# Scatters tied to evictions, a PSUM copy moved to ScalarE and output adds moved later, in a convolution and expert kernel

## The chip, the cores and the metric

The kernel runs on one core of one Trainium2 chip. The metric is the device time of one execution in microseconds. A comparison runs the kernel and the kernel before in turn on the same chip. What differed is the chip, or something that goes with a call on it, and this turned out to matter more than the change: the same kernel before takes about 1382 us in some calls and 1474 to 1501 us in others. On chip 13 it took about 1477 us in both calls; no other chip is known to have been used twice, so chip and call are not fully told apart, and "chip" below stands for either. Absolute times are therefore compared only inside one batch of runs, and ratios only between chips of the same kind.

## The reference

Tokens are 8 sequences of 3584, 192 channels wide. First comes a causal convolution of seven taps with softmax weights, one set for each of eight heads. Then every token goes to one of eight experts: the arg max of its logits, or the expert of the token before if a local gate is 0.5 or more. Output and arithmetic are float32.

```python
h = np.maximum(x[b, s] @ w1[e], 0.0)      # 192 -> 1024
out[b, s] = p[e] * (h @ w2[e])            # 1024 -> 192, times the softmax share
```

## The kernel before

The tokens are cut into 16 groups of 14 x 128. For each group VectorE does the convolution, a *gate round* on TensorE finds the logits, VectorE works out a slot for each token, and 14 *scatters* (indirect DMAs issued by GpSimd) put the rows into a buffer in DRAM, sorted by expert. TensorE works through *blocks* of that buffer: one unit (128 tokens) for the first 35 blocks, then two units, then one unit again. A block is: hidden matmuls, relu, transposes of the next block's tokens, output matmuls into two PSUM tiles, their sum times the gate, and one indirect DMA to the output for each unit.

The parts that the change touches:

```python
def put():                       # one scatter
    ...
    ins = nc.gpsimd.indirect_dma_start(out=slots[:, :], in_=rows, ...)

def turn(n, xg):                 # transposes on TensorE into xps, then
    nc.vector.tensor_copy(to..., at...)        # xT <- xps, on VectorE
    return xT

def output(n, wb, xg, hT):
    ...                          # matmuls into yps[0], yps[1]
    for k in range(n):
        nc.scalar.activation(o_sb[:, k, :], y[0], Act.Copy, scale=gate)
        nc.vector.scalar_tensor_tensor(o_sb[:, k, :], y[1], gate, o_sb[:, k, :],
                                       Alu.mult, Alu.add)
        ...                      # indirect DMA to out

def step(time, scatters):        # a share of the next groups' convolution or routing,
    ...                          # put into the engines' queues here
    for _ in range(scatters):
        put()

for i, (_, n, _, _) in enumerate(blocks):
    ...
    hT = hidden(n, wbs[i], xT)
    if i + 1 < len(blocks):
        xT = turn(blocks[i + 1][1], xgs[i + 1])
    step(2.5 if n == 1 else 4.2, 1)
    output(n, wbs.pop(i), xgs.pop(i), hT)
    step(2.5 if n == 1 else 4.2, n)
```

`step` hands out routing work up to a "hop", where an answer of another engine is needed. The rest of that step is convolution, and the next step goes on after the hop.

## Time and profile before

| | kernel before |
|---|---|
| time, 3 runs without a profile | 1381.68 us (1381.24 to 1384.63) |
| span of the profiled execution | 1474.5 us |
| busy: TensorE, weight loads | 94%, 89% |
| busy: VectorE, ScalarE, GpSimd | 61%, 29%, 33% |

Shares of the span do not say what is worth changing here; the kernel has four stretches with different limits, and the prediction below reads them one by one. The first oddity is the table itself: the profiled execution is 93 us longer than the timed ones.

### The profile page before, as it was taken

To read this page: it belongs to the slowest core of one execution; us is meant where nothing else is said; L and a number is where in the kernel's file an instruction comes from. 1 tells how busy PE (TensorE), PEld (TensorE's weight loads), DVE (VectorE), ACT (ScalarE), POOL (GpSimd) and SP (SyncE) were. 2 spreads that over 40 slices of the span, in tenths; PEclk is the share of its full clock that TensorE was granted. 3 is DMA by queue.
4 is the path that set the end of the run, shared out by engine and by line. 5 is a ranking of instruction groups with operands and counts; after the bars stand their busy time and mean duration, and the time that the engine had idled before them with its cause. 6 is when DMAs were issued, how large, how long until landed. Compare 5 with 4: busy or idle time off the path is not lost.

```text
span 1474.5 us, 41949 instructions
## 1 busy us (share of the span) xinstructions
PE 1393.4 (94%) x17314; PEld 1315.6 (89%) x17314; DVE 896.7 (61%) x2605; ACT 434.6 (29%) x1014; POOL 479.3 (33%) x515
## 2 busy tenths in 40 slices
PE   6689999999999999999999999999999999999998
PEld 4379888889898999898989999899989999999998
DVE  7579888887777878777777777777531111111111
ACT  3223323323233323232332323232222222222332
POOL 1332434333334333333434343434334212111111
PEclk9789999999999999999999999999999999999999
DMA  4397988885656565656565656555556655546894
GB/s 168 137 345 309 349 335 322 318 319 211 246 199 243 208 247 209 240 203 243 202 246 194 250 192 246 199 185 199 186 199 207 216 180 190 199 166 242 315 325 145
DMA packets 66480, 344.13 MB, mean 233 GB/s; under 512 B 12528, under 2 KB 23655, under 8 KB 45810
## 3 DMA queue, kind: packets, MB, share of 16 engines
q1 hardware_dynamic: 44064, 288.76, 55.0%
q0 software_dynamic: 22224, 52.70, 9.4%
q8 instruction: 136, 2.23, 0.6%
q14 instruction: 54, 0.44, 0.1%
q10 hardware_dynamic: 2, 0.00, 0.0%
HBM read 288.61 MB, written 53.49 MB: 232 GB/s over the span
## 4 chain that ended last, share of the span: by engine, by line
PE 58%; issue 23%; DVE 8%; POOL 5%; DMA 2%; another core or an unknown queue 2%; ACT 1%; POOLq 0%; DVEq 0%; SPq 0%; ACTq 0%
PE yps L756 26%; PE hps L741 24%; POOL out_dram L770 4%; DVE y_sb L206 3%; PE hps L350 3%; PE xps L278 2%; POOL slots L566 1%; PE yps L189 1%; PE hps L189 1%; DMA wb<-in_w_dram 1%; DVE xT L727 1%; DVE o_sb L766 1%; DMA out_dram<-o_sb,xg 1%; DMA x_sb<-in_x_dram 0%
## 5 line engine op out<-in xcount | busy, mean ns | idle before, releaser
L756 PE MATMUL yps<-wb,hT 64*128 64x192 f32 x7392 | 672.4, 327 | 23.2 <-issue 19.1
L756 PEld LDWEIGHTS yps<-wb,hT 64*128 64x128 f32 x7392 | 615.3, 188 | 48.4 <-issue 42.7
L741 PE MATMUL hps<-xT,wb 64*128 64x256 f32 (+1 forms) x6912 | 643.0, 337 | 7.8 <-DVE xT L727 5.0
L741 PEld LDWEIGHTS hps<-xT,wb 64*128 64x128 f32 x6912 | 608.6, 188 | 21.8 <-DVE xT L727 9.5
L770 POOL DMA_INDIRECT out_dram<-o_sb,xg x231 | 234.9, 1017 | 854.6 <-DVE o_sb L766 782.8
L206 DVE SCALAR_TENSOR_TENSOR y_sb<-x_sb,c,y_sb 128x336 f32<-128x336 f32 x720 | 402.9, 568 | 20.3 <-ACT y_sb L181 2.5
L746 ACT ACTIVATE hT<-hps 128x512 f32<-128x512 f32 (+1 forms) x576 | 264.9, 510 | 432.6 <-PE hps L741 317.4
L566 POOL DMA_INDIRECT slots<-y_sb,posi x224 | 217.4, 971 | 112.7 <-issue 108.4
L765 ACT ACTIVATE o_sb<-yps,xg 128x192 f32<-128x192 f32 x231 | 87.6, 418 | 503.0 <-PE yps L756 492.4
L766 DVE SCALAR_TENSOR_TENSOR o_sb<-yps,xg,o_sb 128x192 f32<-128x192 f32 x231 | 87.9, 412 | 240.8 <-ACT o_sb L765 233.5
L724 DVE COPY xT<-xps 128x768 f32<-128x768 f32 x87 | 82.8, 952 | 193.4 <-remote 107.6
L278 PEld LDWEIGHTS xps<-ident,xg 64*128 64x128 f32 x1386 | 78.0, 140 | 3.4 <-PE hps L741 0.3
L278 PE MATMUL xps<-ident,xg 64*128 64x64 f32 x1386 | 77.0, 223 | 0.1
L727 DVE COPY xT<-xps 128x384 f32<-128x384 f32 x57 | 31.6, 554 | 64.8 <-PE xps L278 47.3
L181 ACT ACTIVATE y_sb<-x_sb,c 128x336 f32<-128x336 f32 x116 | 64.7, 575 | 0.0
L350 PE MATMUL hps<-z,wg 64*32 64x128 f32 x1344 | 44.7, 286 | 16.0 <-issue 15.7
L350 PEld LDWEIGHTS hps<-z,wg 64*32 64x32 f32 x1344 | 25.5, 110 | 32.0 <-issue 31.1
L366 DVE COPY lt<-lq 32x36 f32<-32x36 f32 x224 | 44.6, 199 | 3.3
L340 DVE STREAM_TRANSPOSE z<-y_sb 128x768 f32<-128x768 f32 (+1 forms) x56 | 44.1, 844 | 0.0
L189 PE MATMUL hps<-x_sb,wb 128*128 128x336 f32 x56 | 17.8, 482 | 3.5 <-DMA x_sb<-in_x_dram 3.5
L189 PEld LDWEIGHTS hps<-x_sb,wb 128*128 128x128 f32 x56 | 11.5, 207 | 9.4 <-issue 4.8
L355 ACT COPY ls<-hps 128x128 f32<-128x128 f32 x28 | 6.1, 269 | 46.7 <-PE hps L350 46.7
(166 smaller groups left out, 367.3 us busy)
## 6 DMA issues: line engine op xcount, KB each, us to landing
wb<-in_w_dram SPq DMA_DIRECT2D x144, 1536.0 KB
x_sb<-in_x_dram SPq DMA_DIRECT2D x16, 1920.0 KB
xg<-slots SPq DMA_DIRECT2D x87, 258.0 KB
xg<-slots SPq DMA_DIRECT2D x57, 129.0 KB
out_dram<-o_sb,xg POOLq DMA_INDIRECT x231
slots<-y_sb,posi POOLq DMA_INDIRECT x224
wg<-in_wgl_dram SPq DMA_DIRECT2D x1, 144.0 KB
slots<-pad SPq DMA_DIRECT2D x1, 129.0 KB
```

Source lines behind the costliest of these rows:

```text
L181: nc.scalar.activation(cols(h), chans(h, 0), Act.Copy, scale=c[:, h, 0:1])
L206: nc.vector.scalar_tensor_tensor(cols(h), chans(h, k), c[:, h, k:k + 1], cols(h), Alu.mult, Alu.add)
L278: nc.tensor.transpose(to, src[rows], identity=ident[rows, rows])
L350: nc.tensor.matmul(lps[half][Q * j:Q * j + Q, :], lhsT=wgq[rows, b, :], rhs=z[rows, begin[j]:begin[j] + TQ, b * Q:(b + 1) * Q], start=(b = ...
L566: ins = nc.gpsimd.indirect_dma_start(out=slots[:, :], in_=rows, in_offset=None, out_offset=bass.IndirectOffsetOnAxis(ap=to, axis=0)).ins
L724: nc.vector.tensor_copy(to.rearrange("p h d k s -> p h (d k) s"), at.rearrange("p h d k s -> p h (d k) s"))
L741: nc.tensor.matmul(hps[half][:, j, w], lhsT=wb[rows, f0:f0 + P], rhs=xT[rows, d, w], start=(d == 0 and j == 0), stop=(d == KD - 1), skip_g ...
L746: nc.scalar.activation(hT[:, m:m + 2, w], hps[half][:, :, w], Act.Relu)
L756: nc.tensor.matmul(yps[half][:, k * D:(k + 1) * D], lhsT=hT[rows, m, k * P:(k + 1) * P], rhs=wb[rows, WA + m * D:WA + (m + 1) * D], start= ...
L765: nc.scalar.activation(o_sb[:, k, :], y[0], Act.Copy, scale=gate)
L766: nc.vector.scalar_tensor_tensor(o_sb[:, k, :], y[1], gate, o_sb[:, k, :], Alu.mult, Alu.add)
L770: sent = nc.gpsimd.indirect_dma_start(out=out, in_=o_sb[:, k, :], in_offset=None, out_offset=bass.IndirectOffsetOnAxis(ap=xg.bitcast(I32)[ ...
```

## The change

Its intent is to keep GpSimd from issuing many scatters in a row, to take the copy off VectorE, and to let VectorE do convolution work while ScalarE evicts the first half of the output. Cut to its core:

```diff
-    def put():
+    def put(behind=None):
...
+        if behind is not None:
+            tc.add_manual_dep(ins, behind.ins.name, SYNC, reason="scatters apart")
...
-            nc.vector.tensor_copy(...)
+        copied = nc.scalar.copy(to, at)
+        return xT, copied
...   # hidden(), after each of the two pairs of relus
+            put(relu)
...   # output()
         for k in range(n):
-            nc.scalar.activation(o_sb[:, k, :], y[0], Act.Copy, scale=gate)
-            nc.vector.scalar_tensor_tensor(o_sb[:, k, :], y[1], gate, o_sb[:, k, :],
+            nc.scalar.activation(o_sb[:, k, :], y[k][0], Act.Copy, scale=xg[:, k, 0:1])
+        step(1.2)
+        for k in range(n):
+            nc.vector.scalar_tensor_tensor(o_sb[:, k, :], y[k][1], ...)
...   # main loop
-            xT = turn(blocks[i + 1][1], xgs[i + 1])
-        step(2.5 if n == 1 else 4.2, 1)
+            xT, copied = turn(blocks[i + 1][1], xgs[i + 1])
+            if len(to_put) > NT // 2 and n == KT:
+                put(copied)
+        step(2.5 if n == 1 else 4.2)
         output(n, wbs.pop(i), xgs.pop(i), hT)
-        step(2.5 if n == 1 else 4.2, n)
+        step(1.3 if n == 1 else 3.0)
```

More of the change, by code (lines that the diff above doesn't have):

```diff
@@ L723, in turn @@
         if n == KT:
-            nc.vector.tensor_copy(to.rearrange("p h d k s -> p h (d k) s"),
-                                  at.rearrange("p h d k s -> p h (d k) s"))
-        else:
-            nc.vector.tensor_copy(to[:, :, :, 0, :], at[:, :, :, 0, :])
-        return xT
+            to, at = [a.rearrange("p h d k s -> p h (d k) s") for a in (to, at)]
+        else:
+            to, at = [a[:, :, :, 0, :] for a in (to, at)]
+        copied = nc.scalar.copy(to, at)
+        return xT, copied
     def hidden(n, wb, xT):
@@ L745, in hidden @@
                 m = half * 4 + two * 2
-                nc.scalar.activation(hT[:, m:m + 2, w], hps[half][:, :, w], Act.Relu)
+                relu = nc.scalar.activation(hT[:, m:m + 2, w], hps[half][:, :, w], Act.Relu)
+            put(relu)
         return hT
@@ L761, in output @@
         o_sb = op.tile([P, KT, D], F32, name="o_sb")
+        y = [[yps[half][:, k * D:(k + 1) * D] for half in range(2)] for k in range(n)]
         for k in range(n):
-            gate = xg[:, k, 0:1]
-            y = [yps[half][:, k * D:(k + 1) * D] for half in range(2)]
-            nc.scalar.activation(o_sb[:, k, :], y[0], Act.Copy, scale=gate)
-            nc.vector.scalar_tensor_tensor(o_sb[:, k, :], y[1], gate, o_sb[:, k, :],
+            nc.scalar.activation(o_sb[:, k, :], y[k][0], Act.Copy, scale=xg[:, k, 0:1])
+        step(1.2)
+        for k in range(n):
+            nc.vector.scalar_tensor_tensor(o_sb[:, k, :], y[k][1], xg[:, k, 0:1], o_sb[:, k, :],
                                            Alu.mult, Alu.add)
@@ L809, in route_op, with step @@
         return c
-    def step(time, scatters):
+    def step(time):
         start_route()
@@ L830, in step @@
                 time -= c
-        for _ in range(scatters):
-            put()
     start_conv(ON_PE)
@@ L870, in ensure @@
                     return
-                step(4.2, 1)
+                step(4.2)
+                put()
             xgs[j] = load_rows(j)
@@ L885 @@
     weights(AHEAD - 1)
-    xT = turn(blocks[0][1], xgs[0])
+    xT, _ = turn(blocks[0][1], xgs[0])
     for i, (_, n, _, _) in enumerate(blocks):
```

## The prediction

> **What bounds the kernel now.** I read the page first, then a table of stretches, then timelines of single blocks. The page's span is 1474.5 us, but the runs without a profile take 1381.68 us: the profiled execution is 93 us longer. Which of its stalls belong to the kernel and which to being profiled is therefore the main question.
>
> The stretches, cut where the blocks change (one unit per block from 80.7 us on, two units with scatters from 321.1, two units without from 1152.2, one unit again from 1346.6). Columns after the stretch: length, busy time (and count) of TensorE matmuls, weight loads, VectorE, ScalarE, GpSimd, then granted clock, DMA share, GB/s.
>
> ```profile
> 80.70:321.10 240.40, 224.91 (x3400) 209.57 (x3402) 202.97 (x584) 78.93 (x220) 92.08 (x93) 0.97 0.89 331
> 321.10:1152.20 831.10, 801.08 (x9520) 758.94 (x9518) 591.44 (x1764) 242.72 (x521) 307.92 (x309) 1.00 0.61 216
> 1152.20:1346.60 194.40, 194.40 (x2231) 193.89 (x2229) 30.20 (x54) 52.25 (x108) 36.00 (x37) 1.00 0.54 188
> 1346.60:1474.50 127.90, 121.57 (x1889) 120.97 (x1885) 21.65 (x45) 38.94 (x112) 23.33 (x24) 0.99 0.75 268
> ```
>
> In the third stretch TensorE has no gap. A block of two units there, from the TensorE timeline:
>
> ```profile
> 1206.26 5.39 PE L741 MATMUL hps<-xT,wb 64*128 64x256 f32 x48
> 1211.44 0.58 PE L278 MATMUL xps<-ident,xg 64*128 64x64 f32 x12
> 1211.81 5.47 PE L756 MATMUL yps<-wb,hT 64*128 64x192 f32 x64
> 1217.07 3.23 PE L741 MATMUL hps<-xT,wb 64*128 64x256 f32 x28
> ```
>
> From start to start it takes 1217.07 - 1206.26 = 10.81 us; the same reading for one unit (1413.23 to 1418.74) gives 5.51 us. These are the floors. The second stretch has 69 two-unit blocks, x 10.81 = 746 us, and ten rounds of gate matmuls (960 of them, 30.7 us busy). The remainder, about 54 us, is stalls. They look like this (a block where VectorE has no other work at all, so that only scatters can matter):
>
> ```profile
> 1095.07 0.98 POOL L770 DMA_INDIRECT out_dram<-o_sb,xg  x1 [5.71 <-DVE o_sb L766]
> 1096.35 0.98 POOL L770 DMA_INDIRECT out_dram<-o_sb,xg  x1 [0.30 <-issue]
> 1097.64 0.97 POOL L566 DMA_INDIRECT slots<-y_sb,posi  x1 [0.30 <-issue]
> ...
> 1098.91 0.96 POOL L566 DMA_INDIRECT slots<-y_sb,posi  x1 [0.30 <-issue]
> ...
> 1100.17 0.96 POOL L566 DMA_INDIRECT slots<-y_sb,posi  x1 [0.30 <-issue]
> 1102.11 3.25 PEld L756 LDWEIGHTS yps<-wb,hT 64*128 64x128 f32 x40 [0.82 <-issue]
> 1102.12 3.53 PE L756 MATMUL yps<-wb,hT 64*128 64x192 f32 x40 [0.39 <-issue]
> 1102.19 0.96 DVE L724 COPY xT<-xps 128x768 f32<-128x768 f32 x1 [7.07 <-remote]
> ```
>
> Five indirect DMAs in a row, then TensorE's weight loads miss 0.82 us and the copy of the transposed tokens, whose transposes ended near 1099.6, starts at 1102.19. That block takes 11.7 us. Blocks with two output DMAs and no scatter keep 10.81. This is what the diff aims at.
>
> But do the runs without a profile have those stalls? Add the floors: 80.7 us of start + the second stretch at its floor, 746 + 10 x 2.5 = 771 us + the last two stretches, 194.4 + 127.9 = 322.3 us. That is 1174 us and leaves 1381.7 - 1174 = 208 us for the first stretch, which needs at least 35 x 5.51 = 193 us of blocks and about 4 x 2.5 = 10 us of gate matmuls, 203 us. The runs without a profile thus have room for next to none of the 54 us; even if the start is 10 us shorter there, only some 15 us are free. I read most of the stalls as brought by the profile.
>
> The first stretch is different: there VectorE is busy 203 of 240 us, and a block is its work. Its timeline over one block:
>
> ```profile
> 95.62 2.85 DVE L206 SCALAR_TENSOR_TENSOR y_sb<-x_sb,c,y_sb 128x336 f32<-128x336 f32 x5
> 95.76 2.95 PE L741 MATMUL hps<-xT,wb 64*128 64x128 f32 x48
> ...
> 98.39 0.41 DVE L766 SCALAR_TENSOR_TENSOR o_sb<-yps,xg,o_sb 128x192 f32<-128x192 f32 x1
> ...
> 98.72 2.85 DVE L206 SCALAR_TENSOR_TENSOR y_sb<-x_sb,c,y_sb 128x336 f32<-128x336 f32 x5
> ...
> 101.49 0.55 DVE L727 COPY xT<-xps 128x384 f32<-128x384 f32 x1
> ...
> 102.09 2.95 PE L741 MATMUL hps<-xT,wb 64*128 64x128 f32 x48 [0.37 <-issue]
> ```
>
> TensorE starts the next block at 102.09, just when the copy ends at 102.04. The period, 6.33 us, is VectorE's queue: 2.85 + 0.41 + 2.85 + 0.55 less overlaps. The copy stands last in it.
>
> **The Trainium skill.** "Perfetto Trace Analysis", section "Identifying the Most-Contended Engine", says matmul busy share overstates TensorE and weight-load share is fairer: here 759 of 831 us in the second stretch against 193.9 of 194.4 in the third, so the scattered stretch does have gaps in the profile. "ScalarE: Activation LUTs", section "What ACT_TABLE_LOAD costs", gives 186 ns + 0.833 ns per element for an ACTIVATE with immediates: 826 ns for 768 elements and 506 for 384. The trace has 595 ns for 512 and 381 for 256 (the relus), a few per cent less than the formula's 612 and 399, so I take 810 and 490 ns. "DMA: Bandwidth & Descriptors", section "Specifications", puts the HBM limit per core near 358 GB/s; the first stretch moved 331 at a share of 0.89. "SBUF — State Buffer", section "Who interferes with whom", says that only two-port VectorE instructions or ones with two SBUF inputs shut GpSimd out; the copy reads PSUM, so by it the move should not change the scatters' own 0.97 us, and the trace gives no sign that it would.
>
> **The change part by part.**
> Copy to ScalarE: VectorE loses 87 x 0.952 + 57 x 0.554 = 114 us in all, 19.7 us of it in the first stretch. ScalarE gains about 87 x 0.81 + 57 x 0.49 = 98 us on 434.6 busy, and is then near 36% of the span. It runs right after the second pair of relus, while TensorE does the output matmuls (2.7 us for one unit, 5.3 for two), so it is off the path.
> Adds of output halves: no operation is added. The convolution steps become 2.5 + 1.2 + 1.3 where they were 2.5 + 2.5, which at 0.6 per operation is 5 + 2 + 3 = 10 as before; for two units 7 + 2 + 5 = 14 as before. VectorE's wait for the ScalarE half (233.5 us, L766 on the page) is filled sooner, but where it is long VectorE is not the bound.
> The two PSUM tiles of the output are freed up to two operations (1.1 us) later; the next output matmuls need them about 3 us after the last ones end, so this hardly delays anything.
> Scatters: still two per one-unit block. In two-unit blocks three while over seven wait, then two: a group's 14 leave over six blocks as 3,3,2,2,2,2, not five as 3,3,3,3,2. Each now waits for a relu or the copy. By the profile a block with two scatters costs 11.0, one with three 11.4 to 12.6; so the profiled span may fall by 20 to 60 us. That is not the time.
>
> In the first stretch a convolution block becomes 10 x 0.566 + 0.41 = 6.07 us at VectorE, where it was 6.33 to 6.58; VectorE's sum falls from 203 to 183 us, below TensorE's 203. But DMA then holds: 240.4 us x 331 GB/s = 79.6 MB, and 331/0.89 = 372 GB/s with no engine ever idle, so 214 us. Since the floors left 208 to 218 us for this stretch, the real runs are already near that. I give 6 us here of the 15 that VectorE alone would allow. For stalls that may be in the real runs after all I give 4 us. Sum: 1381.7 - 6 - 4 = 1372 us.
>
> **Rivals.** (1) The stalls are real without a profile: then up to half of 54 us goes, and the time is near 1350. For it: the scatter pattern is regular and TensorE itself stops. Against it: the sum of floors, which would then exceed the measured time. (2) The first stretch is held by weight transfers: VectorE's relief is worth nothing, time 1378 to 1382. For it: DMA share 0.89. Against it: blocks of 5.52 us occur there. (3) A new wait: the relu-tied scatters finish a block later, row loads come late, or ScalarE in its order holds the relus behind the copy. Time 1385 to 1400. Against it: loads are issued three blocks ahead and the scatters of a group are over before its rows are asked for; ScalarE is two thirds idle.
>
> **Range and chances.** (1) pulls the low end, (2) and (3) the high end: 1356 to 1384. Faster by over 2% means below 1354.6; I give that 0.07. Slower by over 2% needs rival (3) at full size: 0.02.
>
> **What would show it.** In the new profile: ScalarE copies of about 0.81 and 0.49 us; first-stretch convolution blocks near 6.0 us and no wait of TensorE for the copy; no block over 10.81 without scatters; blocks with two scatters near 11; a profiled span that falls more than the time does. A time under 1355 with stalls gone would make my reading of the profile's own share wrong; an unchanged first stretch with DMA at 0.9 would show rival (2).

## The result

| | median of 4 runs | range |
|---|---|---|
| before | 1382.63 us | 1381.24 to 1384.63 |
| after | 1378.54 us | 1376.37 to 1379.59 |

The ratio is 0.9967, with a 95% interval from 0.9949 to 0.9986: a gain of 0.3%, which by the limit of 2% counts as the same. Ratios are the mean time of one kernel's fast runs over that of the other's of the same rounds, so they are not quite the ratios of the medians.

The profiled execution of the kernel after took 1378.85 us, the same as its timed runs, with a span of 1377.1 us. So the two pages cannot be compared line by line: the page of before comes from an execution of 1476.25 us, the page of after from one of 1378.85 us. The stretches of after (length, then busy time and count of TensorE matmuls, weight loads, VectorE, ScalarE, GpSimd, then clock, DMA share, GB/s):

```profile
71.30:290.60 219.30, 210.88 (x3402) 204.92 (x3403) 196.67 (x593) 92.88 (x256) 94.01 (x94) 0.98 0.98 379
290.60:1055.20 764.60, 764.60 (x9518) 724.08 (x9518) 524.09 (x1646) 289.94 (x589) 309.63 (x308) 1.00 0.67 236
1055.20:1249.60 194.40, 194.40 (x2231) 185.36 (x2229) 13.36 (x36) 64.38 (x126) 36.01 (x37) 1.00 0.54 188
1249.60:1377.10 127.50, 121.29 (x1889) 120.99 (x1886) 9.94 (x24) 46.76 (x133) 23.33 (x24) 1.00 0.77 268
```

TensorE now fills the second stretch completely, 764.60 of 764.60 us, where the page of before had 801.08 of 831.10. The last two stretches are as long as they were. The copies, from the groups of ScalarE kept apart by shape (line, operation, shapes, count, busy us, mean ns, idle before):

```profile
L729 ACT COPY xT<-xps 128x768 f32<-128x768 f32 x87 | 70.2, 807 | 0.0
L729 ACT COPY xT<-xps 128x384 f32<-128x384 f32 x57 | 27.7, 487 | 10.4 <-PE xps L278 10.4
```

They took 807 and 487 ns. A two-unit block with three scatters, from the timeline of GpSimd (start, length, engine and line, operation, tiles, count; in brackets the idle time before it and what ended it):

```profile
636.79 0.99 POOL L775 DMA_INDIRECT out_dram<-o_sb,xg  x1 [4.46 <-DVE o_sb L771]
638.08 0.99 POOL L775 DMA_INDIRECT out_dram<-o_sb,xg  x1 [0.31 <-DVE inn L604]
640.14 1.12 POOL L566 DMA_INDIRECT slots<-y_sb,posi  x1 [1.08 <-issue]
642.18 0.96 POOL L566 DMA_INDIRECT slots<-y_sb,posi  x1 [0.92 <-ACT hT L748]
643.44 0.96 POOL L566 DMA_INDIRECT slots<-y_sb,posi  x1 [0.30 <-issue]
```

The row of five is broken into two, one and two, and this block takes 10.81 us, the floor. Read against the page of before, this looks like the success of the scatters. The times say otherwise: 1378.5 against 1382.6.

### The profile page after: what moved, and what is told of

Its sections match the earlier page's. It is cut to its first block, busy times and chain, and to the rows that moved or that the text cites. A ratio compares the mean times of both kernels' runs of the same rounds, so it can differ in the third digit from the quotient of the medians.

```text
span 1377.1 us, 42248 instructions
## 1 busy us (share of the span) xinstructions
PE 1341.6 (97%) x17314; PEld 1267.5 (92%) x17314; DVE 794.8 (58%) x2461; ACT 516.0 (37%) x1158; POOL 483.7 (35%) x515
## 4 chain that ended last, share of the span: by engine, by line
PE 62%; issue 22%; DVE 6%; POOL 4%; DMA 4%; ACT 1%; POOLq 0%; SPq 0%; DVEq 0%; ACTq 0%
PE yps L759 28%; PE hps L743 27%; POOL out_dram L775 4%; DVE y_sb L206 3%; DMA xg<-slots 3%; PE xps L278 2%; PE hps L350 2%; PE hps L189 1%; PE yps L189 1%; POOL slots L566 1%; DVE z L340 1%; DVE o_sb L771 1%; DMA x_sb<-in_x_dram 1%; DMA out_dram<-o_sb,xg 0%; ACT z L307 0%
## 5 line engine op out<-in xcount | busy, mean ns | idle before, releaser
L759 PE MATMUL yps<-wb,hT 64*128 64x192 f32 x7392 | 644.0, 326 | 3.2 <-DVE o_sb L771 1.9
L743 PE MATMUL hps<-xT,wb 64*128 64x256 f32 (+1 forms) x6912 | 635.5, 336 | 0.6 <-ACT xT L729 0.6
L759 PEld LDWEIGHTS yps<-wb,hT 64*128 64x128 f32 x7392 | 606.1, 188 | 8.1 <-issue 4.0
L743 PEld LDWEIGHTS hps<-xT,wb 64*128 64x128 f32 x6912 | 573.7, 188 | 39.8 <-ACT xT L729 0.8
L566 POOL DMA_INDIRECT slots<-y_sb,posi x224 | 223.0, 995 | 185.5 <-ACT hT L748 88.5
L729 ACT COPY xT<-xps 128x768 f32<-128x768 f32 (+1 forms) x144 | 97.9, 680 | 10.4 <-PE xps L278 10.4
L278 PEld LDWEIGHTS xps<-ident,xg 64*128 64x128 f32 x1386 | 71.3, 140 | 12.9 <-issue 2.9
L350 PE MATMUL hps<-z,wg 64*32 64x128 f32 x1344 | 26.9, 274 | 1.9 <-DVE z L340 1.7
L189 PE MATMUL yps<-x_sb,wb 128*128 128x336 f32 x56 | 19.2, 500 | 0.0
L189 PEld LDWEIGHTS yps<-x_sb,wb 128*128 128x128 f32 x56 | 11.6, 215 | 5.4 <-issue 1.3
```

The lines of the kernel that those rows point to most:

```text
L189: nc.tensor.matmul(acc, lhsT=dg_of(i, k), rhs=chans(h, k), start=(k == 0), stop=(k == KC - 1))
L278: nc.tensor.transpose(to, src[rows], identity=ident[rows, rows])
L350: nc.tensor.matmul(lps[half][Q * j:Q * j + Q, :], lhsT=wgq[rows, b, :], rhs=z[rows, begin[j]:begin[j] + TQ, b * Q:(b + 1) * Q], start=(b = ...
L729: copied = nc.scalar.copy(to, at)
L743: nc.tensor.matmul(hps[half][:, j, w], lhsT=wb[rows, f0:f0 + P], rhs=xT[rows, d, w], start=(d == 0 and j == 0), stop=(d == KD - 1), skip_g ...
L759: nc.tensor.matmul(yps[half][:, k * D:(k + 1) * D], lhsT=hT[rows, m, k * P:(k + 1) * P], rhs=wb[rows, WA + m * D:WA + (m + 1) * D], start= ...
```

## The experiments

Three theories of the 93 us, by the letters used in the expectations: **P**, the stalls are brought by profiling (the prediction's); **R**, the profile caught a rare slow execution; **C**, they belong to the chip or placement on which a kernel runs. And two questions on the change: what each part is worth, and where the rest of the forecast 10 us went.

### First batch, chip 13: each part alone

`before_again` is the kernel before, unchanged.

> The kernel before, unchanged, for a second profile and the size of the noise. Theory P (the 93 us by which the profiled run of before was longer than its plain runs are brought by profiling, through runs of scatters): the plain time is 1382 us, ratio 1.00 within 0.2%, and this profile again has a span near 1474 us with blocks of 11.4 to 12.6 us. Rival R (that profiled run was one slow execution that happens now and then): the span of this profile is near 1381 us, with two-unit blocks of 10.81 us although three scatters follow each other.

Measured: 1474.11 us (1472.02 to 1477.9), ratio 0.9984 [0.9964, 1.0004] to the 11 runs of before beside it (median 1477.25). The execution with a profile had a span of 1470.6 us, and the rounds without one are as long. P falls: the timed runs have the stalls too. R falls: all 11 executions have them. C stays.

`copy_only`: the copy on ScalarE, all else as before (the line for one unit; the one for two is changed in the same way).

```diff
-            nc.vector.tensor_copy(to[:, :, :, 0, :], at[:, :, :, 0, :])
+            nc.scalar.copy(to[:, :, :, 0, :], at[:, :, :, 0, :])
```

> Only the copy of the transposed tokens on ScalarE. Theory D (what was gained, 4 us, lies in the first stretch of one-unit blocks: VectorE's queue is relieved there until the DMA engines hold it): this part alone gives nearly all of it, 1378 to 1380 us. Rival S (the scatters' spacing gives the 4 us): 1382 us. In the profile, theory P expects stalls as in before, since the scatters still come in a row: span 1440 us or more; rival R expects about 1378.

Measured: 1467.39 us, 0.9930 [0.9911, 0.9948].

`scatter_only`: the kernel after with the copy back on VectorE and the adds whole.

```diff
-        copied = nc.scalar.copy(to, at)
+        copied = nc.vector.tensor_copy(to, at)
...
-        step(1.2)
-        for k in range(n):
...
-        step(1.3 if n == 1 else 3.0)
+        step(2.5 if n == 1 else 4.2)
```

> Only the scatters tied to the relus and to the (VectorE) copy. Theory D: 1382 us, within 1.5 us of before, as real runs have no stalls from scatters. Rival S: 1378 us. Profile: theory P expects the stalls gone, a span within 10 us of the time; without theory P the span tells nothing.

Measured: 1417.77 us, 0.9597 [0.9578, 0.9616].

`halves_only`: only the moved adds; copy on VectorE, scatters at the ends of the steps.

```diff
-            put(relu)
+            pass
...
-        copied = nc.scalar.copy(to, at)
+        copied = nc.vector.tensor_copy(to, at)
...
-            if len(to_put) > NT // 2 and n == KT:
-                put(copied)
...
+        put()
...
+        for _ in range(n):
+            put()
```

> Only VectorE's adds of output halves behind a short step of other work; the scatters stay in a row. Theory D: VectorE has as much to do as before, but it waits less, so between 1379 and 1383 us. Rival S: 1382 us. Rival H (the adds alone carry the gain): 1378 us. Profile under theory P: stalls as in before, span over 1440 us.

Measured: 1479.73 us, 1.0013 [0.9990, 1.0036]. On this chip the scatters alone are worth 4.0%, the copy 0.7%, the adds nothing.

### Second batch, chip 8: does the weights' transfer hold the first stretch?

`after_again` is the kernel after, unchanged.

> The changed kernel, unchanged. The last four runs overturned theory P: on their chip the kernel before takes 1477 us in eleven plain runs, so the stalls are real there and absent where it took 1382 us. Theory C (a condition of the chip or of the placement in memory makes runs of scatters stall TensorE[...]; the changed kernel does not depend on it because its scatters are apart and the copy no longer queues behind them): where before takes about 1477 us, this takes 1400 to 1418 us; where before takes about 1382 us, this takes about 1378 us. Rival K (the condition only belonged to that one call or program, not to the chip): before is near 1382 us here and the difference 4 us.

Measured: 1393.16 us (1392.15 to 1394.52), 0.9280 [0.9258, 0.9302] to before's 1500.66 us. On this kind of chip the change gains 7.2%, not 0.3%.

`before_halfw` and `after_halfw` load only every second weight tile of the one-unit blocks and use it twice. Their outputs are wrong, which doesn't matter for the times.

```diff
-            wbs[j] = load_w(j)
+            wbs[j] = wbs[j - 1] if j < ONE[-1] and j % 2 else load_w(j)
```

> Wrong on purpose: in the first stretch every second one-unit block uses the weights of the block before it, so about 27 MB of weight loads go away. Theory Q (the DMA engines hold the first stretch, 219 us at 379 GB/s in the changed kernel): before gets faster by 3 to 8 us and is then held by VectorE's queue. Rival V (VectorE alone holds it): no change, within 2 us.

> Wrong on purpose: the changed kernel with the same weights left out. Theory Q: 10 to 15 us faster than the changed kernel, first stretch near 205 us, so the change is worth 10 us or more once the DMA engines do not hold the stretch. Rival V: no faster than the changed kernel by more than 2 us.

Measured: before 1496.53 us, 0.9974 [0.9944, 1.0003]; after 1392.16 us, 0.9269 [0.9243, 0.9296]. The first stretch of `after_again`, then of `after_halfw` (columns as above):

```profile
80.60:305.50 224.90, 215.03 (x3402) 204.68 (x3404) 199.00 (x605) 94.29 (x256) 94.08 (x94) 0.99 0.96 358
```

```profile
80.70:304.50 223.80, 213.44 (x3402) 203.79 (x3404) 198.96 (x605) 94.04 (x256) 94.16 (x94) 0.99 0.67 240
```

A third of the traffic is gone (358 to 240 GB/s), and the stretch is 1.1 us shorter. On this chip, a DMA share of 0.96 does not mean that DMA is the bound.

`after_early2` begins the two-unit blocks after two groups instead of three.

```diff
-EARLY = 3
+EARLY = 2
```

> A version that may beat both: two-unit blocks begin after 21 one-unit blocks instead of 35, which saves 7 weight loads of 1.57 MB, 11 MB, in the stretch held by DMA. Theory Q: 8 to 15 us faster than the changed kernel unless blocks must wait for their tokens. Rival V: no faster, as VectorE's work for the first groups must still be done before their blocks.

Measured: 1403.03 us, 0.9343 [0.9317, 0.9369], 10 us slower than the kernel after. This way to a faster version is closed.

### Third batch, chip 3, where before takes 1381.76 us: undo one part

I call a chip of this kind *quiet* and the other kind *stalling*.

`after_copy_dve` puts the copy back on VectorE (the line shown for `scatter_only`, nothing else).

> The changed kernel with the copy of the transposed tokens back on VectorE (scatters still tied to it where the third one is). Theory C: where the kernel before stalls (1470 us or more), the scatters and the adds keep most of the gain, 1410 to 1420 us, as the scatters alone did (0.9597), and the copy is worth the last 20 us. Rival W (the copy on ScalarE is what makes room, scatters matter only with it): 1440 us or more. Where before takes 1382 us: 1379 to 1383 us.

Measured: 1391.25 us (1390.54 to 1392.16), 1.0072 [1.0056, 1.0089]: 0.7% slower than before, the same by the limit of 2% but clear of the noise. Scatters and adds without the copy cost time.

`after_joint` puts the adds back (the other two edits of `scatter_only`), so it has copy and scatters.

> The changed kernel with the adds of the output halves back right behind their first halves and two steps of work as before. If the adds matter only together with the rest: 10 us or more slower than the changed kernel (1393 us on a stalling chip). If they matter nowhere: within 3 us of it.

Measured: 1374.67 us (1372.88 to 1376.19), 0.9947 [0.9930, 0.9963]. It beats the kernel before. The kernel after was not run in this batch, and its interval (0.9949 to 0.9986) overlaps this one; but the next two kernels, which keep the moved adds, took 3.0 and 4.0 us more on the same chip.

`after_row` puts the scatters of a block in a row behind its first pair of relus.

```diff
-            put(relu)
+            if two == 0:
+                many = 3 if len(to_put) > NT // 2 + 2 and n == KT else 2
+                for _ in range(many):
+                    put(relu)
...
-            if len(to_put) > NT // 2 and n == KT:
-                put(copied)
```

> The changed kernel with as many scatters per block, but all of a block's tied to the first pair of relus, so that they run in a row, behind the output DMAs. Theory C (it is the row that stalls): on a stalling chip blocks with three scatters again take 11.4 us or more and the time rises by 20 us or more over the changed kernel; blocks with two stay near 11. Rival N (only the number per block counts, or the copy's place): within 5 us of the changed kernel. On a chip where before takes 1382 us: no difference.

Measured: 1377.71 us, 0.9969 [0.9952, 0.9986], the same as the kernel after's 0.9967.

`after_spread` leaves only one scatter in most one-unit blocks.

```diff
-            put(relu)
+            if two == 0 or n == KT or len(to_put) > 4 or (to_put and to_put[0][0] < 2):
+                put(relu)
```

> A version that may beat both: in one-unit blocks the second scatter is left out once only four of a group's wait, so there are more blocks with one. Theory C: on a stalling chip, where one-unit blocks with two scatters took 6.06 instead of 5.52 us, about ten blocks gain 0.5 us each, 3 to 6 us faster than the changed kernel. Rival: no faster[...].

Measured: 1378.64 us, 0.9979 [0.9962, 0.9995]: no gain over the kernel after.

What weight loads waited for in the first stretch (engine and tile, releaser: us in all, times, longest), first `after_copy_dve`, then the kernel after, then `after_joint`:

```profile
PEld yps L759 <- DVE o_sb L771: 14.0, 20, 1.5
PEld hps L350 <- DVE z L340: 5.1, 9, 1.0
```

```profile
PEld yps L759 <- DVE o_sb L771: 3.9, 7, 0.9
PEld hps L350 <- DVE z L340: 3.5, 6, 1.0
```

```profile
PEld yps L759 <- DVE o_sb L768: 2.8, 6, 0.6
```

The first line is the PSUM tile that a late add still holds. With the copy on VectorE as well, it costs 14.0 us; with the adds back in place, 2.8 us of it remain. The second is the gate matmuls waiting for VectorE's transposes z. It is gone where the adds are back in place, though the gate matmuls then wait 1.9 us for something that the profile does not name.

### Fourth batch, chip 13 again: copy and scatters on a stalling chip

What was left open after the third batch is which part makes the gain on a quiet chip and whether rows of scatters alone stall on a stalling one.

> The kernel before once more, for a trace of it in this call's condition. If the chip is one of those where it takes about 1382 us, its trace has no idle stretches of TensorE of 2 to 4 us in blocks 35 to 104, that stretch of the run takes about 776 us as in the kernel after, and the first stretch (35 one-unit blocks) about 221 us. If the chip is one of those where it takes 1475 to 1500 us, that stretch takes 840 us or more.

`before_third`, the kernel before unchanged: 1477.96 us, 1.0002 [0.9971, 1.0033]. The chip was a stalling one once more, so this gave no quiet trace of before.

> Only the copy on ScalarE. On a chip where before takes about 1382 us: the copy is worth the most of the change there (taking it away cost the whole 12.7 us), so about 1373 us, ratio 0.993; if instead the copy is only worth something together with the moved scatters, as before, ratio 0.998 to 1.001. On a stalling chip: 0.993 as measured.

`copy_only_b`, the same kernel as `copy_only`: 1466.7 us, 0.9921 [0.9890, 0.9951], as measured before.

> Copy and scatters changed, the adds whole. On a chip where before takes about 1382 us: 1374.7 us as in the run before, ratio 0.995. On a stalling chip: if the moved adds cost what they cost on the undisturbed one, about 4 us less than the kernel after had there, so 1389 us, ratio 0.925; if VectorE's adds don't matter where other stalls do, 1393 us, ratio 0.928.

`joint_b`, the same kernel as `after_joint`: 1405.12 us, 0.9505 [0.9479, 0.9530]. The expected 0.925 or 0.928 failed. Against the 0.928 of the kernel after on chip 8, the adds seem to be worth 2% on a stalling chip. But the two ratios are of different chips, so neither the size nor the cause is settled.

> The kernel after with the scatters in a row again. On a chip where before takes about 1382 us: 1377.7 us as in the run before, ratio 0.997. On a stalling chip it decides: if the row of scatters is what stalls, 1460 to 1475 us, ratio 0.99; if copy and adds take the stalls away too, under 1410 us, ratio 0.94 or less.

`row_b`, the same kernel as `after_row`: 1418.59 us, 0.9596 [0.9570, 0.9622]. It fell between both expectations: rows of two or three behind one relu bring back part of the stalls, while on the quiet chip the same kernel lost nothing.

Blocks 35 to 104 are the two-unit blocks up to the end of the scatters: 60 without and 10 with a gate round. Stalled means longer than 11.0 us without a gate round, where the floor is 10.81:

| kernel (chip) | blocks 35 to 104, us | stalled, of 60 | mean of the gate blocks, us |
|---|---|---|---|
| before_third (13, stalling) | 845.7 | 39 | 15.6 |
| copy_only_b (13) | 840.3 | 42 | 15.4 |
| scatter_only (13) | 786.8 | 1 | 13.8 |
| row_b (13) | 795.2 | 21 | 13.7 |
| joint_b (13) | 786.6 | 1 | 13.7 |
| after_again (8, stalling) | 775.7 | 1 | 12.6 |
| after (quiet) | 775.5 | 0 | 12.7 |

On a stalling chip the scatters remove the ordinary stalls and the copy does not. The kernel after is 10.9 us shorter there than `joint_b`, nearly all of it in the gate blocks (12.6 against 13.7 us each). This need not be the adds: `row_b`, which has them moved too (with its scatters in rows), also takes 13.7 us on chip 13.

Every kernel here, the changed ones too, puts the first group's 14 scatters in one row in the start, and there the kernel after itself can be compared on both kinds of chip. ScalarE's copies of z for the second gate round fall into that row. On the quiet chip, then on chip 8 (`after_again`):

```profile
56.96 3.03 ACT L307 COPY z<-hps 128x512 f32<-128x512 f32 x6
```

```profile
60.25 1.29 ACT L307 COPY z<-hps 128x512 f32<-128x512 f32 x2 [3.65 <-remote]
68.08 2.05 ACT L307 COPY z<-hps 128x512 f32<-128x512 f32 x4 [6.54 <-remote]
```

From the third on, the scatters of the row take 0.96 us each, 0.30 us apart, on both chips, but on chip 8 ScalarE stands still for 3.65 and 6.54 us, for a release whose source the profile does not find ("remote"), and TensorE with it. The row from 48.0 us on ends at 65.9. Across all traces the first block begins at 79.4 to 82.2 us on stalling chips and at 70.7 to 72.2 us on quiet ones. Of the 15.7 us by which the kernel after is longer on chip 8 than on its quiet chip, 9.3 are in this start and 5.6 in the first stretch.

### Fifth batch, chip 1, where before takes 1382.22 us: the missing corners

`copy_halves` is `halves_only` with the copy on ScalarE: copy and adds, with the scatters in the places of before.

> The copy and the moved adds, with the scatters in the places of the kernel before (at the ends of the steps). On an undisturbed chip (before about 1382 us): the order of the scatters is worth nothing there, so the same as the kernel after, 1378 us, ratio 0.997; if the tied scatters are worth the 4 us that the prediction gave them, 1382 us, ratio 1.000. On a stalling chip (before 1475 us or more): if only the scatters count there, as for the copy alone, 1465 us, ratio 0.993; if copy and adds together take stalls away as beside the scatters in rows of three (ratio 0.960), under 1425 us.

Measured: 1377.68 us (1375.93 to 1379.09), 0.9963 [0.9946, 0.9979]. This is what the kernel after has with its tied scatters.

> Only the scatters tied to evictions; copy on VectorE, adds whole. On an undisturbed chip (before about 1382 us): the copy on VectorE cost 16.5 us beside the moved adds and the adds cost 4 us, so 1387 us, ratio 1.004, if the two add up; if the scatters alone are worth something there, under 1378 us, ratio below 0.997. On a stalling chip: 0.960 as measured.

`scatter_only_b`, the same kernel as `scatter_only`: 1382.20 us, 0.9996 [0.9980, 1.0013], exactly the kernel before. On chip 13 the same edit gained 4.0%.

`copy_halves` has before's row of two output DMAs and three scatters. Its timeline of GpSimd in one block:

```profile
635.81 0.98 POOL L775 DMA_INDIRECT out_dram<-o_sb,xg  x1 [8.52 <-DVE o_sb L771]
637.09 0.97 POOL L775 DMA_INDIRECT out_dram<-o_sb,xg  x1 [0.30 <-DVE inn L604]
638.37 0.97 POOL L566 DMA_INDIRECT slots<-y_sb,posi  x1 [0.30 <-issue]
639.64 1.22 POOL L566 DMA_INDIRECT slots<-y_sb,posi  x1 [0.30 <-issue]
641.16 0.96 POOL L566 DMA_INDIRECT slots<-y_sb,posi  x1 [0.30 <-issue]
```

It is the pattern that the prediction showed, five in a row, each 0.3 us after the other. The block takes 10.81 us, and so do all its neighbours without a gate round. On a quiet chip the row costs nothing.

Four kernels in the first stretch (35 one-unit blocks, of which four have a gate round), summed from the blocks of their traces. No trace of the kernel before from a quiet chip was kept; `scatter_only_b`, which takes the same time, stands for it:

| kernel, quiet chips | first stretch, us | its four gate blocks | the other 31 |
|---|---|---|---|
| scatter_only_b | 222.0 | 30.9 | 191.1 |
| after_joint (copy moved) | 214.9 | 32.8 | 182.1 |
| after (adds moved too) | 219.3 | 37.3 | 182.1 |
| copy_halves (after, old scatters) | 218.5 | 37.1 | 181.4 |

The copy takes 9.0 us off the ordinary blocks and gives 1.9 back in the gate blocks. The adds cost 4.4 us, and all of it is in the gate blocks. The kernels are of three quiet chips and one trace each. The copy alone, without tied scatters or moved adds, was never measured on a quiet chip.

## Why the prediction was right or wrong

The time, 1378.54 us, is inside the range, and "within 2%" was right. But of the forecast 10 us only 4 came. Against the kernel before of the same batch the parts are: copy and scatters together -0.53%, about 7 us; scatters alone 0; putting the moved adds on top, +3 us. That leaves 4 us. The forecast had -6 for the first stretch, -4 for residual stalls, and nothing for the adds. So two terms of its sum failed: the 4 us for stalls measured 0, and the 0 for the adds measured +3 us (the kernel after against `after_joint`, by their ratios; 4.4 us between their first stretches). The copy's term was right.

**The copy: right.** Its durations were estimated at 0.81 and 0.49 us and measured at 0.807 and 0.487. That it stood last in VectorE's queue and held the next block is what the trace of `scatter_only_b` shows on a quiet chip, in one block:

```profile
105.45 0.55 DVE L729 COPY xT<-xps 128x384 f32<-128x384 f32 x1
106.05 0.64 PEld L743 LDWEIGHTS hps<-xT,wb 64*128 64x128 f32 x10 [0.69 <-DVE xT L729]
```

In all, its waits on the first stretch:

```profile
PEld hps L743 <- DVE xT L729: 11.3, 19, 0.8
```

With the copy on ScalarE (`after_joint`) this wait is down to 0.8 us, and the first stretch falls from 222.0 to 214.9 us. The prediction said 214 and a gain of 6; the gain was 7.

**DMA as the holder at 214 us: not shown.** The length agrees, and `after_joint` moved 383 GB/s there at a share of 0.98. But on chip 8 a third less traffic changed nothing at a share of 0.96, and ordinary blocks on quiet chips reach 5.51 us, TensorE's floor. No run took traffic away on a quiet chip, so what holds the last microseconds there is open. Rival (2), transfers that make VectorE's relief worthless, is wrong in either case: the copy gained 7 us.

**"This hardly delays anything", of the moved adds: wrong.** Only the free time of the PSUM tiles was looked at, and the wait for those did stay small (3.9 us in the first stretch of the kernel after, 2.8 in `after_joint`). The second effect was missed: a block now has three steps instead of two, so a gate round's pieces land in other places of the queues. This is block 6 of the kernel after, from the timeline:

```profile
113.44 1.84 DVE L340 STREAM_TRANSPOSE z<-y_sb 128x768 f32<-128x768 f32 x2
115.20 0.38 DVE L771 SCALAR_TENSOR_TENSOR o_sb<-yps,xg,o_sb 128x192 f32<-128x192 f32 x1
115.50 1.42 DVE L340 STREAM_TRANSPOSE z<-y_sb 128x768 f32<-128x768 f32 x2
116.51 0.14 PEld L350 LDWEIGHTS hps<-z,wg 64*32 64x32 f32 x4 [1.04 <-DVE z L340]
```

The add of the previous block stands between the transposes, and the gate matmuls wait 1.04 us for the last ones. In `after_joint` the four transposes run together from 115.19 to 118.34 us, its gate matmuls start at 121.15, one block later, and they wait for no z (but once 1.15 us for something that the profile doesn't name). Block 6 takes 11.27 us, of which 5.76 is over an ordinary block; a gate block of `after_joint` takes 7.85 to 8.58. Not all of the 5.76 is this wait: the same block waits for rows (0.67 us) and once for something the profile doesn't name (1.36). That the adds cost 4.5 us in the gate blocks is shown by `after` against `after_joint`; that the order of the pieces causes it is read from the trace and was not tested by itself. In favour of it, the waits for z come to 3.5 us in three of the four gate blocks of the kernel after, and the fourth, without one, takes 7.74 us. The gate rounds also come earlier (blocks 6, 14, 23, 32 instead of 7, 16, 25, 34), so more routing falls into this stretch: VectorE was to fall to 183 us of work there and has 196.67 (593 instructions) in the kernel after, 187.51 (539) in `after_joint`.

**The size of VectorE's block, 6.07 us: right where it shows.** Blocks of 6.03 to 6.12 us occur in the kernel after, where VectorE's backlog has run up to the PSUM tiles (blocks 22 and 29 to 31). Most others take 5.51 to 5.6.

**4 us for stalls in the real runs: wrong; they were 0.** Blocks 35 to 104 take 776.2 us in `scatter_only_b`, 775.5 in the kernel after and 775.5 in `copy_halves` with its rows of five. The sum of floors had said so (771 us for 69 of these 70 blocks, and next to no room), and the 4 us were put on top against it. The term for a gate round, 2.5 us, was too high: on quiet chips a gate block takes 12.7 us, 1.9 over the floor. The 69 blocks take 764.60 us in the kernel after, so the stalls in the page of before were about 66 us (831.10 - 764.60) and not 54.

**"I read most of the stalls as brought by the profile": wrong in the cause.** They are in all executions on stalling chips, with or without a profile. For the forecast the reading did no harm, because the timed runs given for before must, by their 1382 us, have come from a quiet chip, where they are absent. Had the timed runs been from chip 8, rival (1), the stalls are real, would have been right and the forecast far too small: there the change gains 7.2%.

**Scatters 3, 3, 2, 2, 2, 2: right.** Blocks 66 to 71 of the kernel after have just these counts. They have no effect on a quiet chip. Rival (3), a new wait, did come, but as the 4.5 us of the gate blocks and not through the scatters or ScalarE's order.

What stays open is what about a chip makes it stall. The packets of the indirect DMAs' queue took about the same time in both kinds (9.4% of 1474.5 us in before, 10.0% of 1376.3 us in `copy_halves`, about 138 us in each). In the stalled block that the prediction shows, TensorE's weight loads go on at 1102.11 and VectorE's copy at 1102.19, after both had stood still. No run could vary the chip at will.

## What to carry to other kernels

Before you explain a difference between a profile and a time, check that both come from executions of the same length, and look for an execution of the kernel before beside yours: here a part of the change that was worth 4% on one chip was worth nothing on another. When work is moved inside a software schedule, list what else its queue position decides: here the gate rounds moved with the adds, and in their blocks about half of what the copy had won was lost. Take the sum of floors at its word, and add no allowance against it.

On a quiet chip, use the copy and the scatters without the moved adds (`after_joint`, 0.9947); on a stalling one the kernel after has the lowest ratio of a correct kernel (0.9280 on chip 8), but `after_joint` was measured on another stalling chip (0.9505 on chip 13), so the two are not ranked there.

## What the Trainium skill lacked or had wrong

- "DMA: Bandwidth & Descriptors", section "Specifications", puts the HBM limit per core near 358 GB/s. The row does not say that this is the share of a core whose neighbour streams too; further down, under "Measured (HBM→SBUF, 128 partitions, SWDGE, issued from GpSimd)", the same page does. This program runs on one core, and the row is no ceiling for it: `after_joint` moved 383 GB/s over 215 us of its first stretch and the kernel after 379 GB/s over 219 us.
- "Perfetto Trace Analysis", section "Identifying the Most-Contended Engine", names the weight-load share, with the share of peak FLOPs, as the measure of how close TensorE is to roofline, and does not say how exact it is. In 172.92 us of blocks 105 to 120, in which TensorE's matmuls have no gap, the weight loads of the kernel after were busy 164.89 us in one execution and 172.46 us in another (`after_again`): a share of 0.95 was no gap.
- None of the pages read says that a chip can differ from another on the same one-core kernel: 1382 us on chips 1 and 3, 1477 on chip 13, 1501 on chip 8, each repeated within 1% in a batch. Nor does one say that rows of indirect DMAs can go with stalls of the other engines on one chip and not on another: `scatter_only` took 1417.77 us against 1477.25 on chip 13, and the same kernel (`scatter_only_b`) 1382.20 against 1382.22 on chip 1.
